# Strassen's seven products for eight in the second layer's first product, its split weights kept in HBM

## The chip, the cores and the metric

One core of a Trainium2 chip runs the whole program. The metric is device time in microseconds from one launch to its end: the median of three runs was 867.01 us, the lowest 866.56, the highest 867.7. Beside these there is one profiled execution, whose trace has a span of 865.0 us.

## The reference, cut to what matters

```python
scores = scale * np.matmul(q, k.transpose(0, 1, 3, 2))          # 4 batches, 8 heads, 576 tokens, 64 wide
ret = scores * Dmat[None, :, :, :]                              # decay gamma ** (i - j) below the diagonal
x = np.matmul(ret, v) -> 2304 tokens x 512
h = x @ w_in;   g = np.maximum(0.01 * h, h);            x = g @ w_out      # first layer, 512 -> 2048 -> 512
h = x @ w_in2;  g = h * (1.0 / (1.0 + np.exp(-h)));     out = g @ w_out2   # second layer, same sizes
```

All is float32 (the weights arrive as float64). Each layer is two products of 2304 x 512 x 2048.

## The kernel before

Three stages follow one another on TensorE: retention for the eight units of `UNITS` (its small matmuls are woven into the first layer), the first layer, the second layer. Every large product is done in three passes (`PASSES`): each float32 operand is split into a high part `hi`, a rounded float32r copy written by ScalarE (line 113), and a low part, source minus `hi`, written by VectorE (line 114). The passes hi*hi, hi*lo and lo*hi are added in PSUM.

A layer goes through blocks of tokens (`BLOCKS`), and in a block through the 16 tiles `f` of 128 hidden units; one (block, f) is a step. In a step `gemm1` makes `h` (128 hidden units x n tokens) from 4 chunks of 128 inputs in 3 passes: 12 matmuls with n columns each. `activate` applies the nonlinearity and splits the result into `g`. Two steps later (`LAG`) `gemm2` multiplies it with the second weight matrix into `acc`. In the first layer the output is transposed (hidden weights stationary, n columns); in the second layer `g` is stationary and each matmul has 512 columns of weights: 3 passes for each 128 tokens, 12 in a step of 512 tokens. The second layer's blocks are four of 512 tokens and one of 256.

The weights are split again for each block (`split_wi`, `split_wo`), from float32 copies `wraw` that stay in SBUF. These come from the float64 input by `load_w` (two DMAs of 512 KB for one f) and `decode` (ScalarE line 369, VectorE lines 374, 384 and 390). The second layer's weights are loaded and decoded during the last block of the first layer.

The order on every engine is written out by hand up to step 32 (`tc.manual_schedule()`); from there a list scheduler of the framework orders every engine's instructions. PSUM has eight banks: two for `ps` (the tiles `h`), four for `acc`, two for `att`. All DMAs are issued from SyncE's one queue, in order.

Of the kernel before, what the change touches and what calls it, by code (L numbers as in the profile page):

```python
# [21 lines left out]
W2 = 26  # L22
# [5 lines left out]
FIXED = 2 * NF  # L28
CA, CB = 256, S - 256
# [13 lines left out]
for _u in UNITS:  # L43
    POS[_u] = _p
    _p += CA if _u[0] == "A" else CB
BLOCKS = [[(0, 512), (512, 320), (832, 512), (1344, 512), (1856, 448)],
          [(0, 512), (512, 512), (1024, 512), (1536, 512), (2048, 256)]]
# [15 lines left out]
def retention_mlp_kernel(ctx: ExitStack, tc: tile.TileContext, qkva, qkvb, w1, w2, consts, out):  # L63
    nc = tc.nc

    def pool(name, bufs, space=None):
        kw = {"space": space} if space is not None else {}
        return ctx.enter_context(tc.tile_pool(name=name, bufs=bufs, **kw))

    const = pool("const", 1)  # L70
    wraw_p = pool("wraw", 16)
    wi_p = pool("wi", 2)
    wo_p = pool("wo", 2)
    x_p = pool("x", 1)
    xs_p = pool("xs", 6)
    hs_p = pool("hs", 2)
    g_p = pool("g", 3)
    ld_p = pool("ld", 3)
    dec_p = pool("dec", 3)
    pt_p = pool("pt", 4)  # L80
    y_p = pool("y", 2)
    st_p = pool("st", 4)
    acc_p = pool("acc", 1, PSUM)
    att_p = pool("att", 1, PSUM)
    ps_p = pool("ps", 2, PSUM)

# [13 lines left out]
    mask2 = wraw_p.tile([128, H, 128], F32, tag="wraw", name="mask2")  # L100
# [33 lines left out]
    def mm(out, lhsT, rhs, start, stop):  # L134
        return nc.tensor.matmul(out, lhsT, rhs, start=start, stop=stop)  # L135
# [13 lines left out]
    def load(u, p):  # L149
# [6 lines left out]
        if u in UNITS[:2]:  # L156

            t = wraw_p.tile([128, m], F32, tag="wraw", name="qkvk")
# [185 lines left out]
    def load_w(layer, f, parts=(0, 1)):  # L344

        if (layer, f) not in w64:
            p, tag = (ld_p, "ld") if layer == 1 and f < 2 else (wraw_p, "wraw")
            wraw[layer, f] = p.tile([128, 1024], F32, tag=tag, name="wraw")
            w64[layer, f] = dec_p.tile([128, 1024, 2], I32, tag="w64", name="w64")
# [77 lines left out]
    def activate(layer, i, f):  # L427
# [6 lines left out]
        if layer == 0:  # L434
            yield nc.scalar.activation(out=hs[:, :n], in_=h[:, :n], func=AF.Prelu, alpha=0.01)  # L435
        else:
            yield nc.scalar.activation(out=hs[:, :n], in_=h[:, :n], func=AF.Sigmoid)  # L437
            yield nc.vector.tensor_tensor(out=hs[:, :n], in0=h[:, :n], in1=hs[:, :n], op=ALU.mult)  # L438
        yield from split(g[:, 0, :n], g[:, 1, :n], hs[:, :n], nc.vector)

    def gemm2(layer, i, f):
        p0, n = BLOCKS[layer][i]
        nt = KC if layer == 0 else n // 128
        if f == 0:
            t = [acc_p.tile([128, 2, 512], F32, tag=f"acc{m}", name=f"acc{m}") for m in range(2)]

            acc[layer, i] = [t[m // 2][:, m % 2] if nt > 2 else t[m][:, 0] for m in range(nt)]
        g, w = gs[layer, i, f], wsp[layer, i, f, 1]
        for m in range(nt):
            a = acc[layer, i][m]  # L450
            ms = slice(m * 128, (m + 1) * 128)
            for wa, ga in PASSES:
                st = f == 0 and (wa, ga) == (0, 0)
                sp = f == NF - 1 and (wa, ga) == PASSES[-1]
                if layer == 0:
# [134 lines left out]
    for t, (l, i, f) in enumerate(steps):  # L590
# [53 lines left out]
        else:  # L644
# [3 lines left out]
            if t + 2 < len(steps):  # L648
                run(split_wi(*steps[t + 2]))
# [77 lines left out]
```

## Time and profile before

| | |
|---|---|
| median of 3 runs | 867.01 us (866.56 to 867.7) |
| span of the profiled execution | 865.0 us |
| TensorE busy | 855.0 us, 5736 matmuls |
| VectorE busy | 538.0 us |
| ScalarE busy | 443.7 us |
| granted TensorE clock | 0.999 |
| read from HBM, written | 53.11 MB, 4.72 MB |

The chain of waits is the one to start with: it follows the end of the program back, and says which engine held it up. Then the groups of instructions by shape give the number of matmuls, and the timeline gives the distance between the starts of two runs of them, which is what one costs in a stream: the mean duration of a matmul overlaps with the next. The same holds for VectorE and ScalarE: an instruction of 0.69 us may be followed by the next one after 0.60 us.

### The profile page before, as it was taken

The numbers are of one execution on the slowest core, as the hardware profiler recorded it, in microseconds if no ns is written. First come the engines' busy times: TensorE is split into PE (matmuls) and PEld (weight loads), VectorE is DVE, ScalarE is ACT, GpSimd is POOL, SyncE is SP. The second block draws the span as 40 slices with busy tenths as digits, with TensorE's granted clock in tenths as the row PEclk, the third lists the DMA queues.
The fourth block names the chain that finished last, engine by engine and source line by source line (L and its number), as shares of the span: only waits on it lengthen the run. The fifth ranks groups of instructions, "written<-read, shape, count | busy, mean of one in ns | idle before, by whom it ended". The sixth has DMA issues, their size and how long they took to land.

```text
span 865.0 us, 14049 instructions
## 1 busy us (share of the span) xinstructions
PE 855.0 (99%) x5736; PEld 714.8 (83%) x5736; DVE 538.0 (62%) x909; ACT 443.7 (51%) x769; POOL 17.1 (2%) x34
## 2 busy tenths in 40 slices
PE   8999999999999999999999999999999999999998
PEld 5678889998877878889998888888888888888897
DVE  6898856675454564548998444654465446544575
ACT  3788744454343444456666444544454445444564
POOL 5100000000000000000000000000000000000000
PEclk9999999999999999999999999999999999999999
DMA  9767532111111020102660000000001000100000
GB/s 342 275 217 258 168 109 90 58 66 58 50 57 66 1 82 1 49 1 97 231 207 1 2 0 1 25 25 0 1 21 29 1 0 12 38 1 0 25 26 25
DMA packets 17824, 58.73 MB, mean 68 GB/s; under 512 B 2016, under 2 KB 2144, under 8 KB 17760
## 3 DMA queue, kind: packets, MB, share of 16 engines
q1 hardware_dynamic: 17760, 57.83, 19.0%
q8 instruction: 45, 0.74, 0.3%
q14 instruction: 19, 0.16, 0.1%
HBM read 53.11 MB, written 4.72 MB: 67 GB/s over the span
## 4 chain that ended last, share of the span: by engine, by line
PE 93%; DVE 1%; ACT 0%; issue 0%
PE acc L135 45%; PE h L135 44%; PE o L135 2%; PE r L135 2%; DVE st L279 0%; DVE y L471 0%; DVE g L114 0%; ACT g L113 0%; DVE wi L114 0%; DVE wo L114 0%; ACT hs L435 0%; DVE xs L114 0%; DVE pt L204 0%; ACT xs L113 0%; DVE wraw L387 0%
## 5 line engine op out<-in xcount | busy, mean ns | idle before, releaser
L135 PE MATMUL h<-xs,wi 128*128 128x512 f32 (+3 forms) x1920 | 429.6, 370 | 1.8 <-ACT wi L113 1.1
L135 PEld LDWEIGHTS h<-xs,wi 128*128 128x128 f32 x1920 | 340.5, 188 | 62.1 <-ACT wi L113 2.1
L135 PE MATMUL acc<-g,wo 128*128 128x512 f32 (+2 forms) x960 | 216.1, 371 | 0.2 <-DVE wo L114 0.2
L135 PE MATMUL acc<-wo,g 128*128 128x512 f32 x864 | 209.9, 389 | 0.0
L135 PEld LDWEIGHTS acc<-g,wo 128*128 128x128 f32 x960 | 171.8, 188 | 27.0 <-DVE wo L114 0.6
L135 PEld LDWEIGHTS acc<-wo,g 128*128 128x128 f32 x864 | 161.0, 188 | 32.6
L113 ACT CAST wo<-wraw 128x512 fp32r<-128x512 f32 x160 | 99.5, 622 | 116.9 <-PE acc L135 115.8
L114 DVE TENSOR_TENSOR wo<-wraw,wo 128x512 fp32r<-128x512 f32 x160 | 110.4, 690 | 78.5 <-ACT wo L113 77.9
L114 DVE TENSOR_TENSOR wi<-wraw,wi 128x512 fp32r<-128x512 f32 x158 | 108.5, 686 | 56.4 <-ACT wi L113 54.3
L438 DVE TENSOR_TENSOR hs<-h,hs 128x512 f32<-128x512 f32 (+1 forms) x80 | 51.1, 639 | 119.0 <-ACT hs L437 118.9
L114 DVE TENSOR_TENSOR g<-hs,g 128x512 fp32r<-128x512 f32 (+3 forms) x160 | 101.6, 635 | 15.3 <-ACT g L113 10.6
L437 ACT ACTIVATE hs<-h 128x512 f32<-128x512 f32 (+1 forms) x80 | 44.5, 556 | 129.7 <-PE h L135 129.4
L113 ACT CAST wi<-wraw 128x512 fp32r<-128x512 f32 x160 | 98.2, 614 | 13.4 <-DVE wraw L390 13.4
L113 ACT CAST g<-hs 128x512 fp32r<-128x512 f32 (+3 forms) x160 | 93.6, 585 | 15.3 <-DVE hs L438 14.7
L435 ACT ACTIVATE hs<-h 128x512 f32<-128x512 f32 (+2 forms) x80 | 44.3, 553 | 101.0 <-PE h L135 100.1
L369 ACT ACTIVATE wraw<-w 128x1024 f32<-128x1024 f32 (+1 forms) x35 | 36.9, 1059 | 19.4 <-DVE wo L114 12.0
L374 DVE TENSOR_SCALAR w<-w 128x512 uint16<-128x512 uint32 (+1 forms) x34 | 35.7, 1051 | 9.0 <-ACT wraw L369 8.2
L390 DVE SCALAR_TENSOR_TENSOR wraw<-w,wraw 128x1024 int32<-128x1024 int32 (+1 forms) x35 | 39.6, 1131 | 1.3 <-ACT w L380 0.7
L113 ACT CAST xs<-X 128x512 fp32r<-128x512 f32 (+3 forms) x42 | 22.9, 561 | 3.4 <-DVE X L322 2.3
L114 DVE TENSOR_TENSOR xs<-X,xs 128x512 fp32r<-128x512 f32 (+3 forms) x38 | 22.9, 618 | 2.4 <-ACT xs L113 2.2
L380 ACT ACTIVATE w<-w,seven 128x512 uint16<-128x512 uint32 x14 | 20.5, 1463 | 0.0
L384 DVE TENSOR_SCALAR wraw<-wraw 128x512 int32<-128x512 int32 (+1 forms) x34 | 20.1, 590 | 0.0
(57 smaller groups left out, 233.5 us busy)
## 6 DMA issues: line engine op xcount, KB each, us to landing
w<-in_w SPq DMA_DIRECT2D x64, 512.0 KB, 4.7
qkv<-in_qkvb SPq DMA_DIRECT2D x16, 672.0 KB, 6.3
qkvk<-in_qkva SPq DMA_DIRECT2D x16, 256.0 KB, 5.4
qkv<-in_qkva SPq DMA_DIRECT2D x8, 512.0 KB, 4.2
out<-y SPq DMA_DIRECT2D x15, 256.0 KB, 2.0
out<-y SPq DMA_DIRECT2D x6, 128.0 KB, 2.3
cst<-in_consts SPq DMA_DIRECT2D x1, 150.0 KB, 2.3
```

The costliest lines, as they stand in the source:

```text
L113: yield nc.scalar.copy(out=hi, in_=src)
L114: yield engine.tensor_tensor(out=lo, in0=src, in1=hi.bitcast(F32), op=ALU.subtract)
L135: return nc.tensor.matmul(out, lhsT, rhs, start=start, stop=stop)
L369: yield nc.scalar.mul(out=w, in_=hi.bitcast(F32), mul=2.0 ** -112)
L374: yield nc.vector.tensor_scalar(out=end[:, c], in0=lo[:, c].bitcast(U32), scalar1=2.0 ** -29, scalar2=7.0, op0=ALU.mult, op1=ALU.min)
L380: yield nc.scalar.activation(out=end[:, c], in_=lo[:, c].bitcast(U32), func=AF.Relu, scale=-2.0 ** -29, bias=seven)
L384: nc.vector.tensor_scalar(out=wi[:, c], in0=wi[:, c], scalar1=3, scalar2=None, op0=ALU.logical_shift_left)
L390: yield nc.vector.scalar_tensor_tensor(out=wi, in0=hi, scalar=-0x7FFFFFF9, in1=wi, op0=ALU.bitwise_and, op1=ALU.bitwise_xor)
L435: yield nc.scalar.activation(out=hs[:, :n], in_=h[:, :n], func=AF.Prelu, alpha=0.01)
L437: yield nc.scalar.activation(out=hs[:, :n], in_=h[:, :n], func=AF.Sigmoid)
L438: yield nc.vector.tensor_tensor(out=hs[:, :n], in0=h[:, :n], in1=hs[:, :n], op=ALU.mult)
```

## The change

The second layer's first product is done on pairs of 384 tokens (three pairs, `PAIRS`) and pairs of hidden tiles (k = 0 to 7, each two tiles f). The 512 inputs are two halves. That is a product of 2x2 blocks by 2x2 blocks, which needs eight block products in the plain way; the change does it in seven, by the Winograd form of Strassen's scheme. A block product is 2 chunks x 3 passes = 6 matmuls of 384 columns (`product`), so a pair k takes 42 of them (`quad`) where the plain way would take 48.

Four sums of token blocks (`sums_x`, for each pair of token blocks) and four sums of weight blocks (`sums_w`, once for each k) are new, and seven split token operands and seven split weight operands. The split weights of all k, and the split second weights, are written to a scratch tensor in HBM (`kept`, 2.88 MB for each k) while the first pair of token blocks is worked on, and read back for the other two pairs (`fetch`, `weights_out`).

The four results are made in two PSUM tiles, `a` and `b`: after the first, second and third product of the chain in `a`, ScalarE copies it out (`snapshot`) and VectorE adds `b` to the copy (`add`); `finish` applies Silu in place of Sigmoid and a product, and splits. Between the block products the matmuls of the second product of the pair before are placed (`left`, one group of three matmuls for each 128 tokens; `yield 3` means three such groups). In the first quad there are none.

The outputs of a pair (6 tiles of 128 tokens) are gathered in six banks. PE's and SP's order is written out by hand in the second layer, the others' is the scheduler's. The second layer's weights come later: seven f during the last seven steps of the first layer, the other nine during the first pair. Pools are opened and closed so that the new tiles take the place of old ones.

```diff
+TILE = 384
+PAIRS = B * S // (2 * TILE)
-          [(0, 512), (512, 512), (1024, 512), (1536, 512), (2048, 256)]]
...
+    def sums_x(p):
+        t1, t2, t4 = (xt_p.tile([128, 2, TILE], F32, tag="xt", name="xt") for _ in range(3))
+        yield nc.vector.tensor_tensor(out=t1, in0=b12, in1=b11, op=ALU.subtract)
...
+        for name, x in (("b11", b11), ("b21", b21), ("t2", t2), ("t1", t1), ("t3", b12), ("t4", t4), ("b22", b22)):
+            yield nc.scalar.copy(out=hi, in_=x)
+            yield nc.vector.tensor_tensor(out=lo, in0=x, in1=hi.bitcast(F32), op=ALU.subtract)
...
+    dram = pool("scratch", 1, bass.MemoryType.DRAM)
+    kept = {k: dram.tile([128, 22, 256], F32, tag=f"kept{k}", name="kept") for k in range(NF // 2)}
+    PARTS = (("ha", 0, 3), ("la", 3, 3), ("hs", 6, 4), ("ls", 10, 4))
...
+    def weights_out(p, k):
+            if p:
+                nc.sync.dma_start(out=here, in_=there)
+            else:
+                yield from split(wo[i][:, 0], wo[i][:, 1], wraw[1, 2 * k + i][:, 512:], nc.vector)
+                nc.sync.dma_start(out=there, in_=here)
+
+    def fetch(p, k):
+        for n, o, m in PARTS:
+            nc.sync.dma_start(out=t[n].bitcast(F32), in_=kept[k][:, o:o + m])
...
+    def sums_w(p, k):
+        yield nc.scalar.copy(out=ha[:, :2], in_=a)
+        yield nc.vector.tensor_tensor(out=la[:, :2], in0=a, in1=ha[:, :2].bitcast(F32), op=ALU.subtract)
+        yield nc.vector.tensor_tensor(out=s1, in0=z[:, :256], in1=z[:, 256:512], op=ALU.add)
+        yield nc.vector.tensor_tensor(out=s2, in0=s1, in1=w[:, :256], op=ALU.subtract)
+        yield nc.scalar.copy(out=hs[:, :2], in_=s[0])
+        yield nc.vector.tensor_tensor(out=ls[:, :2], in0=s[0], in1=hs[:, :2].bitcast(F32), op=ALU.subtract)
...
+        for n, o, m in PARTS:
+            nc.sync.dma_start(out=kept[k][:, o:o + m], in_=t[n].bitcast(F32))
+
+    def product(out, p, k, a, b, start, stop):
+        w, x = ww[p, k, a], xw[p, b]
+        for c in range(2):
+            for i, (e, f) in enumerate(PASSES):
+                mm(out, w[e][:, c * 128:(c + 1) * 128], x[f][:, c], start and c == 0 and i == 0,
+                   c == 1 and i == len(PASSES) - 1, skip_group_check=True)
+
+    def finish(p, k, f, t, h):
+        with tc.high_priority():
+            nc.scalar.activation(out=g, in_=h, func=AF.Silu)
+            nc.scalar.copy(out=hi, in_=g)
+            nc.vector.tensor_tensor(out=lo, in0=g, in1=hi.bitcast(F32), op=ALU.subtract)
...
+    def quad(p, k):
+        product(a, p, k, "a11", "b11", True, False)
+        c11 = snapshot()
+        product(b, p, k, "a12", "b21", True, True)
+        add(c11)
+        finish(p, k, 0, 0, c11)
+        yield 3
+        product(a, p, k, "s2", "t2", False, False)
+        c12 = snapshot()
+        yield 2
+        product(b, p, k, "s1", "t1", True, False)
+        product(a, p, k, "s3", "t3", False, False)
+        c22 = snapshot()
+        add(c22)
+        finish(p, k, 1, 1, c22)
+        yield 3
+        product(a, p, k, "a22", "t4", False, True)
+        finish(p, k, 1, 0, a)
+        product(b, p, k, "s4", "b22", False, True)
+        add(c12)
+        finish(p, k, 0, 1, c12)
+        yield 4
...
+    later.enter_context(tc.manual_schedule(engines={mybir.EngineType.PE, mybir.EngineType.SP}))
+    for p in range(PAIRS):
+        for k in range(NF // 2):
+            if after[0] == 0:
+                more = sums_w(*after)
+            elif after[0] < PAIRS:
+                fetch(*after)
...
+            if p == 0:
+                more_weights(nw + (2 if k < 4 else 1))
+            left = outputs(p, k)
```

ScalarE at the turn from the first layer to the second. Before, the table of Sigmoid is loaded and the step goes on as the steps before it (`hs<-h` is the nonlinearity, `wi`, `wo` and `g` are the hi copies of splits, `X<-acc` an eviction of the first layer):

```order
L113 CAST wo<-wraw 128x512
L437 ACT_TABLE_LOAD
L437 ACTIVATE hs<-h 128x512
L113 CAST wi<-wraw 128x512
L113 CAST wo<-wraw 128x512
L113 CAST g<-hs 128x512
L437 ACTIVATE hs<-h 128x512
```

Now (`X<-a` is a snapshot, or where it is ACTIVATE a Silu that reads PSUM; `X<-X` is Silu on a copy; `gh` is the hi part of the result):

```order
L581 COPY X<-a 128x384
L566 ACT_TABLE_LOAD
L566 ACTIVATE X<-X 128x384
L467 COPY X<-acc_4178 128x448
L567 CAST gh<-X 128x384
L467 COPY X<-acc_4179 128x448
L121 CAST wo<-wraw 128x512 x4
L581 COPY X<-a 128x384 x2
L566 ACTIVATE X<-X 128x384
L567 CAST gh<-X 128x384
L566 ACTIVATE X<-a 128x384
L567 CAST gh<-X 128x384
```

The second and third snapshot of the first quad stand behind the table load, two evictions of the first layer and four copies of second weights.

TensorE at the same place. Before, runs of 12 matmuls of either product alternate in the second layer:

```order
L135 MATMUL h<-xs,wi 128x512 x12
L135 MATMUL acc_5505<-wo,g 128x512 x6
L135 MATMUL acc_5506<-wo,g 128x512 x6
L135 MATMUL h<-xs,wi 128x512 x12
L135 MATMUL acc_5505<-wo,g 128x512 x6
```

Now, in the first quad (`a`, `b`: block products; `xh`, `xl` and `ha`, `la`, `hs`, `ls`: hi and lo of token and weight operands; `acc<-g,wo`: the last of the first layer):

```order
L143 MATMUL b<-xl,ha 128x384
L143 MATMUL acc_4178<-g,wo 128x448 x2
L143 MATMUL acc_4179<-g,wo 128x448 x2
L143 MATMUL b<-xh,la 128x384
L143 MATMUL acc_4178<-g,wo 128x448 x4
L143 MATMUL acc_4179<-g,wo 128x448 x4
L143 MATMUL a<-xh,hs 128x384
L143 MATMUL a<-xl,hs 128x384
L143 MATMUL a<-xh,ls 128x384
```

From the product on `a` that begins there, 30 matmuls of block products follow with no others between them, then the second quad's first 12.

VectorE in the loaded part. Before, in the last block of the first layer, a decode (lines 374, 384, 390) stands between the lo parts of the splits:

```order
L114 TENSOR_TENSOR g<-hs,g 128x448
L374 TENSOR_SCALAR w_4907<-w_4907 128x1024
L384 TENSOR_SCALAR wraw<-wraw 128x1024
L114 TENSOR_TENSOR wo<-wraw,wo 128x512
L390 SCALAR_TENSOR_TENSOR wraw<-w_4907,wraw 128x1024
L374 TENSOR_SCALAR w_4989<-w_4989 128x1024
L384 TENSOR_SCALAR wraw<-wraw 128x1024
L114 TENSOR_TENSOR wi<-wraw,wi 128x512
```

Now, in the fourth quad of the first pair, from one `add` (line 586) to the next (`ws` are sums of weights, `la` lo parts of weights, `gl` lo parts of results; lines 381, 391 and 397 a decode):

```order
L586 TENSOR_TENSOR X<-b,X 128x384
L538 TENSOR_TENSOR ws<-wraw 128x256
L542 TENSOR_TENSOR ws<-wraw 128x256
L381 TENSOR_SCALAR w_5077<-w_5077 128x1024
L391 TENSOR_SCALAR wraw<-wraw 128x1024
L568 TENSOR_TENSOR gl<-X,gh 128x384
L547 TENSOR_TENSOR la<-wraw,ha 128x256
L539 TENSOR_TENSOR ws<-ws,wraw 128x256
L122 TENSOR_TENSOR wo<-wraw,wo 128x512
L568 TENSOR_TENSOR gl<-X,gh 128x384
L397 SCALAR_TENSOR_TENSOR wraw<-w_5077,wraw 128x1024
L586 TENSOR_TENSOR X<-b,X 128x384
```

Ten instructions of other work stand between two adds for which TensorE waits.

## Rows read from the trace of the kernel before

**Rows 1.** Page: busy time by engine; clock and bandwidth in 40 slices

```profile
PE 855.0 (99%) x5736; PEld 714.8 (83%) x5736; DVE 538.0 (62%) x909; ACT 443.7 (51%) x769; POOL 17.1 (2%) x34
...
PEclk9999999999999999999999999999999999999999
...
GB/s 342 275 217 258 168 109 90 58 66 58 50 57 66 1 82 1 49 1 97 231 207 1 2 0 1 25 25 0 1 21 29 1 0 12 38 1 0 25 26 25
```

**Rows 2.** Page: the chain that ended last, share of the span by engine

```profile
PE 93%; DVE 1%; ACT 0%; issue 0%
```

**Rows 3.** Groups by shape, TensorE: busy us, mean ns; idle before

```profile
L135 PE MATMUL h<-xs,wi 128*128 128x512 f32 x1344 | 329.4, 392 | 1.6 <-ACT wi L113 1.1 <-DVE xs L114 0.5
L135 PE MATMUL acc<-wo,g 128*128 128x512 f32 x864 | 209.9, 389 | 0.0
L135 PE MATMUL h<-xs,wi 128*128 128x256 f32 x192 | 25.8, 282 | 0.0
```

**Rows 4.** Timeline, TensorE, second layer: start us, us, engine, line, shapes, count

```profile
484.02 2.88 PE L135 MATMUL h<-xs,wi 128*128 128x512 f32 x12
486.74 2.88 PE L135 MATMUL acc<-wo,g 128*128 128x512 f32 x12
489.46 2.88 PE L135 MATMUL h<-xs,wi 128*128 128x512 f32 x12
```

**Rows 5.** Timeline, TensorE, blocks of 448 and of 256 tokens

```profile
394.66 5.03 PE L135 MATMUL h<-xs,wi 128*128 128x448 f32 x24
399.52 0.77 PE L135 MATMUL acc<-g,wo 128*128 128x448 f32 x3
...
838.48 1.59 PE L135 MATMUL h<-xs,wi 128*128 128x256 f32 x12
839.91 1.55 PE L135 MATMUL acc<-wo,g 128*128 128x512 f32 x6
841.30 1.59 PE L135 MATMUL h<-xs,wi 128*128 128x256 f32 x12
```

**Rows 6.** Timeline, VectorE, last block of the first layer

```profile
434.75 1.34 DVE L374 TENSOR_SCALAR w<-w 128x1024 uint16<-128x1024 uint32 x1
435.88 0.73 DVE L384 TENSOR_SCALAR wraw<-wraw 128x1024 int32<-128x1024 int32 x1
436.53 0.67 DVE L114 TENSOR_TENSOR wo<-wraw,wo 128x512 fp32r<-128x512 f32 x1
437.12 1.21 DVE L390 SCALAR_TENSOR_TENSOR wraw<-w,wraw 128x1024 int32<-128x1024 int32 x1
```

**Rows 7.** Groups by shape, VectorE and ScalarE

```profile
L114 DVE TENSOR_TENSOR wi<-wraw,wi 128x512 fp32r<-128x512 f32 x158 | 108.5, 686 | 56.4 <-ACT wi L113 54.3
L204 DVE TENSOR_TENSOR pt<-r,mask 128x384 f32<-128x384 f32 x16 | 8.8, 553 | 0.7 <-PE r L135 0.7
L438 DVE TENSOR_TENSOR hs<-h,hs 128x256 f32<-128x256 f32 x16 | 6.8, 424 | 6.9 <-ACT hs L437 6.8
...
L437 ACT ACTIVATE hs<-h 128x256 f32<-128x256 f32 x16 | 6.2, 385 | 10.5 <-PE h L135 10.5
```

**Rows 8.** Busy time by engine in stretches of 10 us; clock, DMA share, GB/s

```profile
413.00:423.00 10.00, 10.00 (x51) 9.28 (x50) 9.47 (x13) 6.55 (x11) 0.00 (x0) 1.00 0.80 283
433.00:443.00 10.00, 10.00 (x51) 9.27 (x50) 9.82 (x13) 6.30 (x10) 0.00 (x0) 1.00 0.64 218
```

**Rows 9.** Timeline, ScalarE, at the turn between the layers

```profile
463.69 1.28 ACT L437 ACT_TABLE_LOAD   x1
467.34 0.60 ACT L437 ACTIVATE hs<-h 128x512 f32<-128x512 f32 x1 [2.36 <-PE h L135]
467.83 0.61 ACT L113 CAST wi<-wraw 128x512 fp32r<-128x512 f32 x1
468.34 0.62 ACT L113 CAST wo<-wraw 128x512 fp32r<-128x512 f32 x1
```

**Rows 10.** Page: DMA issues, KB each, median us from issue to landing

```profile
w<-in_w SPq DMA_DIRECT2D x64, 512.0 KB, 4.7
...
out<-y SPq DMA_DIRECT2D x15, 256.0 KB, 2.0
```

More of the change, by code (lines that the diff above doesn't have):

```diff
@@ L85, in retention_mlp_kernel, with slot @@
     ps_p = pool("ps", 2, PSUM)
+    def slot(shape, dt, name, kind="wraw"):
+        return wraw_p.tile(shape, dt, tag=kind, name=name, bufs={"wraw": NF - 7, "first": 7}[kind])
     cst = const.tile([128, NC + NP * CH], F32, name="cst")
@@ L433, in activate @@
         gs[layer, i, f] = g
[L434 to L438, printed above, removed]
+        yield nc.scalar.activation(out=hs[:, :n], in_=h[:, :n], func=AF.Prelu, alpha=0.01)
         yield from split(g[:, 0, :n], g[:, 1, :n], hs[:, :n], nc.vector)
@@ new lines, in retention_mlp_kernel, with temp, snapshot, add @@
+    temps = itertools.cycle([X[:, c, i * TILE:(i + 1) * TILE] for c in range(2) for i in range(2)])
+    def temp():
+        return next(temps)
+    def quad(p, k):
+        def snapshot():
+            s = temp()
+            with tc.high_priority():
+                nc.scalar.copy(out=s, in_=a)
+            return s
+        def add(s):
+            with tc.high_priority():
+                nc.vector.tensor_tensor(out=s, in0=b, in1=s, op=ALU.add)
+        a = ps_p.tile([128, 512], F32, tag="ps", name="a")[:, :TILE]
+        b = ps_p.tile([128, 512], F32, tag="ps", name="b")[:, :TILE]
+        product(a, p, k, "a11", "b11", True, False)
[19 more added lines that the diff above has]
+        yield 4
@@ L644, in retention_mlp_kernel @@
         else:
-            if t >= t0 - 2:
-                more_weights(NF + 1 + (t - t0 + 2) * 15 // W2)
+            if t >= t0:
+                more_weights(NF + max(0, min(t - t0 - 6, NF - 9)))
                 decodes()
+            if t == t0:
+                heads.close()
+                xh_p = pool("xh", 7, side=right, stack=second)
+                xt_p = pool("xt", 3, side=right, stack=second)
+                x0 = sums_x(0)
+            if t >= t0 + 6:
+                for _ in range(3):
+                    next(x0, None)
+            if t == t0 + NF - 4:
+                run(x0)
+                w0 = sums_w(0, 0)
+            if t >= t0 + NF - 4:
+                for _ in range(4):
+                    next(w0, None)
             if t + 2 < len(steps):
```

177 lines of the change are left out of this document (135 added, 42 removed).

## The prediction

> **What bounds the kernel now.** I read the page's busy times first, then the chain of waits, then the groups by shape, and last the timelines of the stretches that give a price. TensorE is busy for 855.0 of 865.0 us, at the full granted clock in every slice [rows 1], and the chain that ended last lies on TensorE for 93% [rows 2]. A busy TensorE proves little by itself, since its matmuls overlap; the proof is in the groups and the timeline. The second layer's matmuls show next to no idle time before them: 0.0 us before the 864 of the second product, 1.6 us before all 1344 of the 512-column form of the first [rows 3]. And the starts stand at equal distances: runs of 12 begin at 484.02, 486.74 and 489.46, so a matmul of 512 columns costs 2.72 / 12 = 226.7 ns in the stream, whichever product it is of [rows 4]. So what is taken away from TensorE comes off the end, as long as nobody makes it wait.
>
> **What the change removes from TensorE.** Before, the first product of the second layer is 4 x 192 matmuls of 512 columns and 192 of 256. The latter cost (839.91 - 838.48) / 12 = 119.2 ns [rows 5]. 768 x 0.2267 + 192 x 0.1192 = 174.1 + 22.9 = 197.0 us. Now there are 3 pairs x 8 k x 42 = 1008 matmuls of 384 columns, a form that the trace doesn't show. It shows 448 columns at (399.52 - 394.66) / 24 = 202.5 ns and 256 at 119.2 [rows 5]; on the line between these two 384 is 174.7 ns, on the line between 256 and 512 it is 172.9. I take 174: 175.4 us, between 174.3 and 176.1. The gain is 21.6 us, give or take 1. The second product keeps its 864 matmuls of 512 columns. A quad (one pair, one k) is then 42 x 0.174 + 36 x 0.2267 = 7.31 + 8.16 = 15.47 us of TensorE, and the layer is 24 of them.
>
> [...]
>
> **What it adds, and what covers it.**
>
> *The start of the layer.* In the first quad there are no matmuls of a second product to lie between the block products, so each hand-over is open. I count from the end of the first block product (0). The second one ends at 1.85 us (6 x 0.174 and 4 of 448 columns between), 8 more of 448 follow to 3.5, then s2t2 to 4.5 and s1t1 to 5.55. The next, s3t3, writes on `a` and needs the second snapshot. On ScalarE this stands behind the first snapshot, the table load (1.28 us [rows 9]), Silu, which waits for the first add (2.5), two evictions, one gh and four copies of 512. A copy of 512 follows the next after 0.51 us [rows 9]; ACTIVATE on 384 is about 0.49, the middle of 0.385 for 256 and 0.60 for 512 [rows 7, 9], and 0.1 less when the next follows at once; Silu isn't in the trace and is taken as Sigmoid, which these rows are of. That gives Silu to 3.0, evictions and gh to 4.3, four copies to 6.4, the snapshot to 6.9: TensorE waits 1.35 us. After s3t3 (7.95) the third snapshot is open too: 0.55 us. a22t4 and s4b22 then run to 10.6. The second quad's weights `ha` stand on ScalarE behind two Silus and two gh, which puts them at 11.5 (0.9 us of waiting), and their lo part `la` on VectorE behind an add and a gl, at 12.45 (another 0.6). Together 3.4 us. Bounds: 1.5, if the scheduler's order leaves ScalarE ahead of where I put it, and 8, if each of the ten hand-overs costs 0.4 us more.
>
> *The last block of the first layer.* Seven decodes, the split of the first sums of tokens and the first two sums of weights now stand there. In its last eight steps (8 x 24 x 0.2025 = 38.9 us of TensorE) VectorE has seven decodes of 1.13 + 0.65 + 1.21 = 3.0 us [rows 6], 8 x (0.59 + 0.59 + 0.53) us of splits and some 5 us of sums: 39.7 us. So it is full. The block before the change was full as well, 9.82 of 10 us, with TensorE at 10.00 of 10 [rows 8]. I take 0.5 us, from 0 to 3.
>
> *The first pair, quads 2 to 8.* VectorE has for each quad four sums and one lo part of 256, three lo parts of 512, two of second weights, two decodes (in four of the quads), four gl and three adds of 384. By the distances between starts (0.59 for 512 [rows 6], and 0.1 under the mean durations 0.553 for 384 and 0.424 for 256 [rows 7]) that is 1.6 + 1.8 + 1.2 + 6.0 + 3.15 = 13.7 us; by the mean durations (0.686 for 512 [rows 7], 3.28 for a decode) it is 16.0. TensorE's quad is 15.47. So VectorE is 89% full if its work comes in a stream, and the bound if every instruction waits for the one before. TensorE asks for two adds in good time only: from the third block product to s1t1, and from the third snapshot to s4b22, there are some 3 us each. I take 1 us in all, from 0 to 12: the stretch of rows 8 is the nearest row, with TensorE unhurt beside a VectorE at 9.8 of 10. In pairs 2 and 3 the sums of weights and the decodes are gone and VectorE is at 7 us or less; the sums of the next pair's tokens (11 instructions of 768, about 0.87 us each by the same slope) come in one quad each, 3.15 + 9.6 us, and fit.
>
> *DMA.* The first pair writes 2.88 MB for each quad, and in four quads reads 2.10 MB of float64 weights beside it: 4.98 MB in 15.47 us, 322 GB/s. The next pairs read 2.88 MB, 186 GB/s. The trace shows 342 GB/s in the first slice [rows 1] and 283 GB/s at a share of 0.80 [rows 8], so some 350 at full load, all of it reading; writing shows only in pieces of 256 KB that land after 2.0 us [rows 10]. SP issues in order, and each quad's weight loads stand behind the stores of the sums. In quad 2 the first decode on ScalarE comes about when its load lands, with 1.83 MB of stores ahead of it, and a Silu for which TensorE waits stands behind it: 0.5 us, from 0 to 3. Later loads have some 9 us to spare: they are issued 8 us into a quad, and their decode stands 8 us into the next one.
>
> The Trainium skill's page "SBUF — State Buffer", section "The DMA setup-cost knee", speaks against stores of 0.39 and 0.52 MB: about 2 us go to each transfer besides its bytes. One after the other, six stores and four loads would take some 31 us by its figures, twice a quad, and the kernel would come to about 920 us. The trace does not agree that they queue so: 512 KB loads land after 4.7 us [rows 10], which in turn would be 112 GB/s, while 283 were moved [rows 8].
>
> *The end.* The last quad's second product has 36 matmuls with nothing between them, and the same two evictions and stores end the program. I count no change.
>
> **The sum.** 865.0 - 21.6 + 3.4 + 0.5 + 1.0 + 0.5 = 848.8 us of span. The median of the runs, 867.01, is 2.0 above the span of the profiled execution, so the forecast is 850.8, rounded to 851.0 us.
>
> **Rivals.**
> - *Nothing waits.* All stops but a fraction are hidden by the scheduler's order: 867.0 - 21.6 = 845.4 us. For it: the full VectorE of rows 8 cost nothing. Against it: the second snapshot stands behind work that I could name.
> - *VectorE becomes the bound of the first pair.* The adds stand in a strict order among the sums, and each of them waits for TensorE or for a ScalarE copy. With mean durations (16.0) and four waits of 0.5 us a quad takes 18 us, 2.5 more than TensorE; over five quads 12.5 us: 863 us. For it: ten instructions stand between two adds. Against it: rows 6 and 8.
> - *Slower: stores to HBM.* If writing goes at half the rate of reading (177 GB/s for 354), a quad of the first pair needs 2.88 / 0.177 + 2.10 / 0.354 = 22.2 us in four quads, 6.7 too many, and 16.3 in three: 29 us, less 9 to spare, 20: 871 us. ScalarE then waits at its decode for the load, and Silu and the snapshots behind it. It decides from a first pair 16 us longer than I say. For it: no row shows writing in bulk. Against it: the 2.0 us of the small stores.
>
> **How the numbers follow.** The forecast (847 to 856) has 0.54, no waiting 0.20, VectorE 0.16, the stores 0.10. What a measurement of this kernel can tell from no change is 0.2%, 1.7 us: faster is under 865.3, slower over 868.7. Faster: 0.54 + 0.20 + 0.12 of VectorE's 0.16 = 0.86. Slower: 0.08 of the stores' and 0.01 of VectorE's = 0.09. The rest, 0.05, is within. The range goes from 845.0, just under the case without waits, to 864.0, which holds most of VectorE's.
>
> **What would show it.** The block products' starts: 6 x 0.174 = 1.04 us from one run to the next, where nothing waits. TensorE's gaps: after s1t1 and s3t3 of the first quad and at the start of the second, 3.4 us together, the first two ended by ScalarE. Quads 3 to 8 at 15.5 us and those of pairs 2 and 3 at 15.5 without gaps. A first pair with quads of 17 us or more whose gaps are ended by VectorE would speak for that rival; ScalarE waiting at its decode for a load, or a median time to landing of the stores above 8 us, for the slower one. The granted clock should stay at 1.00: if it doesn't in the first quads, the stops were longer than worked out. It would be wrong from the ground up if a 384-column matmul cost 195 ns or more: then the gain is nothing.

## The result

The changed kernel takes 856.45 us (median of 4 runs, 855.64 to 858.67) against 866.96 us for the kernel before. The ratio is 0.988, with a 95% interval of 0.9866 to 0.9894. The forecast was 851.0 us, so the sign was right, the time lies in the range of 845.0 to 864.0, and the gain is 10.5 us where 16.0 were forecast. By the profiled executions it is 854.4 us of span where the sum said 848.8: 5.6 us too few. Most of this document is on where these 5.6 us are.

### The profile page after: what moved, and what is told of

It reads as the page before. It is cut to its first block, busy times and chain, and to the rows that moved or that the text cites. A ratio compares the mean times of both kernels' runs of the same rounds, so it can differ in the third digit from the quotient of the medians.

```text
span 854.4 us, 14185 instructions
## 1 busy us (share of the span) xinstructions
PE 837.3 (98%) x5784; PEld 724.2 (85%) x5784; DVE 479.2 (56%) x850; ACT 423.1 (50%) x762; POOL 16.8 (2%) x34
## 4 chain that ended last, share of the span: by engine, by line
PE 87%; DVE 3%; DMA 2%; ACT 1%; SPq 0%; issue 0%; DVEq 0%; ACTq 0%
PE acc L143 36%; PE h L143 21%; PE a L143 11%; PE b L143 8%; PE att L143 7%; PE o L143 2%; PE r L143 2%; DMA qkv<-in_qkvb 1%; DMA w<-in_w 1%; SPq L359 0%; DVE wraw L397 0%; DVE w L381 0%; DVE gl L568 0%; ACT wo L121 0%; DVE wo L122 0%
## 5 line engine op out<-in xcount | busy, mean ns | idle before, releaser
L143 PE MATMUL h<-xs,wi 128*128 128x512 f32 (+2 forms) x960 | 218.6, 373 | 2.5 <-ACT wi L121 1.7
L143 PEld LDWEIGHTS h<-xs,wi 128*128 128x128 f32 x960 | 171.0, 188 | 31.6 <-ACT wi L121 2.7
L143 PE MATMUL acc<-wo,gh 128*128 128x512 f32 x384 | 134.0, 390 | 0.0
L122 DVE TENSOR_TENSOR wi<-wraw,wi 128x512 fp32r<-128x512 f32 x78 | 53.7, 689 | 63.1 <-ACT wi L121 61.9
L143 PEld LDWEIGHTS acc<-wo,gh 128*128 128x128 f32 x384 | 72.1, 188 | 12.9
L568 DVE TENSOR_TENSOR gl<-X,gh 128x384 fp32r<-128x384 f32 x96 | 53.4, 556 | 45.4 <-ACT gh L567 45.4
L143 PE MATMUL acc<-wo,gl 128*128 128x512 f32 x192 | 75.3, 392 | 0.8 <-DVE gl L568 0.8
L143 PE MATMUL att<-wo,gh 128*128 128x512 f32 x192 | 70.8, 390 | 0.0
L122 DVE TENSOR_TENSOR g<-hs,g 128x512 fp32r<-128x512 f32 (+2 forms) x80 | 50.5, 631 | 9.2 <-ACT g L121 9.2
L567 ACT CAST gh<-X 128x384 fp32r<-128x384 f32 x96 | 49.1, 513 | 2.5
L376 ACT ACTIVATE wraw<-w 128x1024 f32<-128x1024 f32 (+1 forms) x35 | 36.8, 1055 | 10.5 <-DMA w<-in_w 6.3
```

The costliest lines, as they stand in the source:

```text
L122: yield engine.tensor_tensor(out=lo, in0=src, in1=hi.bitcast(F32), op=ALU.subtract)
L376: yield nc.scalar.mul(out=w, in_=hi.bitcast(F32), mul=2.0 ** -112)
L567: nc.scalar.copy(out=hi, in_=g)
L568: nc.vector.tensor_tensor(out=lo, in0=g, in1=hi.bitcast(F32), op=ALU.subtract)
```

## The profile after

The page of the changed kernel: busy time, clock and bandwidth in 40 slices, and the chain that ended last.

```profile
PE 837.3 (98%) x5784; PEld 724.2 (85%) x5784; DVE 479.2 (56%) x850; ACT 423.1 (50%) x762; POOL 16.8 (2%) x34
...
PEclk9999999999999999999999999999999999999999
...
GB/s 338 277 223 242 175 114 107 59 66 58 50 58 66 2 33 2 1 0 1 1 185 99 209 398 363 285 195 212 213 234 169 170 234 140 272 207 138 227 92 74
...
PE 87%; DVE 3%; DMA 2%; ACT 1%; SPq 0%; issue 0%; DVEq 0%; ACTq 0%
```

TensorE lost 17.7 us of busy time against [rows 1] and is the bound still, at the same clock. The chain lies on it for 87% where it was 93% [rows 2]. VectorE, the DMA and ScalarE have taken a few per cent of the chain. The layer's slices (the last 18) now move 138 to 398 GB/s, and 92 and 74 at the end, where all of them moved under 40.

The chain of waits of the changed kernel in one quad (start us, us, what):

```profile
521.99 1.36 PE acc L143 x6
523.35 1.05 PE a L143 x6
524.40 1.05 PE b L143 x6
525.46 1.38 PE acc L143 x6
526.83 1.36 PE att L143 x6
...
537.58 0.45 PE acc L143 x2
```

A block product of six 384-column matmuls costs 1.05 us. The mean distance from one start to the next, stops left out, is 175.4 ns over the whole layer; the line between [rows 5] had said 174. A quad is 537.58 - 521.99 = 15.59 us, where 15.47 was worked out. The products make up 42 x 0.1754 = 7.37 of it, and 8.22 us are left for 36 matmuls of 512 columns: 228.3 ns each, not the 226.7 of [rows 4]. Both are about 1% above the price taken. The lines show where the second comes from: six matmuls of 512 columns right behind a block product take 1.38 us, and the six behind those 1.36, which is the 226.7 ns of [rows 4].

Busy time of the changed kernel by engine in three quads of the first pair (PE, PEld, DVE, ACT, POOL; then clock, DMA share, GB/s), the answer to [rows 8]:

```profile
490.50:506.00 15.50, 14.71 (x74) 13.02 (x73) 13.55 (x22) 9.25 (x18) 0.00 (x0) 1.00 1.03 390
506.00:522.00 16.00, 16.00 (x81) 14.48 (x80) 14.81 (x24) 11.30 (x21) 0.00 (x0) 1.00 1.03 413
522.00:537.60 15.60, 15.60 (x79) 14.14 (x79) 14.44 (x25) 10.27 (x19) 0.00 (x0) 1.00 0.94 343
```

VectorE is up to 93% full and the DMA is at its limit, and yet TensorE has no gap in the second and third of these rows. Where it does stop in the whole layer is a short list. The changed kernel's timeline of TensorE, with the idle time before an instruction and its releaser in brackets, the neighbours of the first stop, and the last matmul of all:

```profile
472.57 0.34 PE L143 MATMUL b<-xh,ls 128*128 128x384 f32 x1
474.18 0.45 PE L143 MATMUL a<-xh,hs 128*128 128x384 f32 x1 [1.27 <-ACT X L581]
474.46 0.34 PE L143 MATMUL a<-xl,hs 128*128 128x384 f32 x1
...
476.07 0.45 PE L143 MATMUL a<-xh,ha 128*128 128x384 f32 x1 [0.57 <-ACT X L581]
479.22 0.44 PE L143 MATMUL a<-xh,ha 128*128 128x384 f32 x1 [0.78 <-ACT ha L534]
480.19 0.44 PE L143 MATMUL a<-xh,la 128*128 128x384 f32 x1 [0.36 <-DVE la L535]
502.18 0.50 PE L143 MATMUL acc<-wo,gl 128*128 128x512 f32 x1 [0.79 <-DVE gl L568]
...
847.70 0.39 PE L143 MATMUL att<-wo,gh 128*128 128x512 f32 x1
```

The first four stops are the hand-overs that the prediction named, in its order and with its releasers: second snapshot, third snapshot, `ha`, `la`. A stop costs more than its idle time. From 472.57 to 474.46 are 1.89 us, where two matmuls in the stream take 0.35: 1.54 us lost for 1.27 us of idle time. Idle time is counted from the end of the matmul before, 0.34 us after its start, while in the stream the next one starts after 0.175; and behind the stop the next start comes 0.28 us later. That is some 0.27 us for each stop, and the four stops cost 4.1 us for 2.98 us of idle time. The fifth stop is in the second quad. The changed kernel's chain of waits there begins at a weight slice that lands late:

```profile
484.32 6.57 DMA w<-in_w
...
490.98 1.14 ACT wraw L376
...
501.66 0.48 DVE gl L568
```

The slice was issued at 483.09 behind stores of the split sums, and its decode set VectorE's order back until `gl` came late. Transfers take longer than before; of the changed kernel's DMA issues (KB each, us to landing):

```profile
w<-in_w SPq DMA_DIRECT2D x64, 512.0 KB, 5.6
```

where the weight slices took 4.7 [rows 10]. At the end, the changed kernel's sync queue issues eight stores:

```profile
846.02 0.34 SPq L636 DMA_DIRECT2D out<-y  x1
846.74 1.11 SPq L636 DMA_DIRECT2D out<-X  x2
847.95 1.73 SPq L636 DMA_DIRECT2D out<-y  x3
849.77 0.54 SPq L636 DMA_DIRECT2D out<-X  x1
850.40 0.40 SPq L636 DMA_DIRECT2D out<-y  x1
```

and the kernel before issued two there:

```profile
861.31 0.89 SPq L476 DMA_DIRECT2D out<-y  x2
```

Before, the span ended 3.9 us after the last matmul (861.13 to 865.0); now it ends 6.3 us after it (848.1 to 854.4). VectorE's last eviction, in the changed kernel and in the kernel before:

```profile
848.74 0.69 DVE L465 COPY y<-att 128x512 f32<-128x512 f32 x1 [0.66 <-ACT X L467]
861.15 0.69 DVE L471 COPY y<-acc 128x512 f32<-128x512 f32 x1 [1.33 <-PE acc L135]
```

Now it waits for ScalarE's eviction of the other block in its PSUM tile and starts 0.6 us after the last matmul; before, it started right at the last matmul's end.

## The experiments

Theory: TensorE sets the pace of the layer, and the 5.6 us are in the price of a matmul, in stops at named places and in the end. Rivals: VectorE or ScalarE set the pace of the first pair; or the traffic to HBM costs time all along.

The first product of the layer starts between 462.9 and 464.7 us in the changed kernel and its variants (e3_vector left out, whose additions begin earlier), and its place is at 462.75 in the kernel before. So up to 2 us of a single profile are the run's own. For small effects I therefore also give the time from that start to the end of the span, which is 390.7 us for the changed kernel; it is called "the layer" below. The sets of runs were taken at different times, and the kernel before took 866.96 to 868.82 us beside them; so differences of 1 to 2 us between the medians of two sets rest on the traces, not on the times alone.

### e1_eighth: an eighth product

```diff
+        product(b, p, k, "s4", "b22", False, False)
         product(b, p, k, "s4", "b22", False, True)
```

> In each of the 24 quads the seventh product (s4 by b22) is done twice, so a quad has eight block products again; left as they are: the quad's sums, evictions and outputs (the output block it feeds holds that product twice). Theory (TensorE alone sets the quad's pitch, other engines follow): 24 quads x 6 matmuls x 0.175 us = 25.2 us more, about 881.6 us, quad pitch 15.59 + 1.05 = 16.64 us, and the stops at the start of the layer unchanged. Rival (VectorE, ScalarE or the DMA set the pace of quads 2 to 8, and TensorE had slack there that the profile does not show as idle time): the first 8 quads take little of it, 17 us or less in all, about 873 us.

879.77 us, 23.3 more than the changed kernel, and 1.4% above the kernel before (1.0124 to 1.0155). The quad's pitch, from one quad's start to the next, is 16.64 us (609.29 to 625.93 in its chain), as expected to the hundredth. The stop in the second quad is gone, presumably since the other engines now have 1 us more for each quad; at the start of that quad there is one stop of 0.89 us of idle time instead of two with 1.14 together; and the span ends 5.9 us after the last matmul instead of 6.3. With the stops at their full cost that is 25.2 - 1.1 - 0.4 = 23.7, and the layer grew by 23.8. The theory held: a block product more costs its full 1.05 us.

### e2_no_kept: no stores and reloads

```diff
-        for n, o, m in PARTS:
-            nc.sync.dma_start(out=kept[k][:, o:o + m], in_=t[n].bitcast(F32))
```

(the store of the output weights and all reloads go likewise)

> The split weights are neither stored in HBM nor reloaded; pairs 2 and 3 multiply with the split weights of the first pair's last two quads, so their part of the result uses other weights; every matmul, sum and eviction stays. Theory (the traffic is hidden except for the one stop of 0.79 us in the second quad, where a weight slice lands late): 0.5 to 1.2 us less, about 855.5 us; the stops at the start of the layer and the pitch of 15.59 us stay. Rival (stores and reloads take time from the matmuls all along, or hold back the end): 5 us or more less, 851 us or below.

867.93 us: 11.5 slower, which neither theory had. ScalarE's timeline of this kernel at the start of the layer:

```profile
467.70 1.13 ACT L376 ACTIVATE wraw<-w 128x1024 f32<-128x1024 f32 x1 [2.95 <-DMA w<-in_w]
...
472.92 1.13 ACT L376 ACTIVATE wraw<-w 128x1024 f32<-128x1024 f32 x1 [3.72 <-DMA w<-in_w]
...
479.12 0.47 ACT L575 COPY X<-a 128x384 f32<-128x384 f32 x1
```

With the sync queue empty, weight loads were issued at 462.13, 466.81 and 472.04 us, where the changed kernel issues the next one at 483.09, and the scheduler put their decodes into the first quad, ahead of the snapshots. ScalarE works in order, so the second snapshot (479.12, where it was 473.65) stood behind a decode that waited for its transfer, and TensorE stopped for 5.8 us; the clock fell behind the stop, which the last section shows. The run says nothing on the traffic: the edit changed the order on an engine that it didn't touch. It does show what the slower rival of the prediction described, ScalarE waiting at a decode with snapshots behind it.

### e3_vector: five more additions a quad

```diff
+            for _ in range(5):
+                yield nc.vector.tensor_tensor(
+                    out=spare, in0=wraw[1, 2 * k][:, :512], in1=wraw[1, 2 * k][:, 512:], op=ALU.add)
```

> Five more VectorE additions of 128 x 512 (about 0.6 us each, 3.0 us a quad, never read) in each of the first pair's eight quads. Theory (VectorE was busy 13.9 to 14.7 of 15.6 us in quads 2 to 5 and less later, with queues between it and TensorE): each of the full quads goes over by about 1.3 to 2.1 us, the later ones have room, and part is caught up: 3 to 10 us more, about 862 us, stops of TensorE on VectorE in quads 3 to 6. Rival 1 (an in-order VectorE already binds; all extra work is felt): 24 us more, about 880 us. Rival 2 (it has slack that the busy time hides, since the end of one instruction overlaps the start of the next): no change, 856.5 us.

869.02 us, 12.6 more: half of the 24 us of work came out at the end, above the theory's 3 to 10. TensorE stopped for 7.6 us in all on the sums, the longest time here:

```profile
533.80 0.56 PE L143 MATMUL b<-xh,hs 128*128 128x384 f32 x1 [2.90 <-DVE X L586]
```

and it ran at a lower clock after two of the stops (0.78 of full in 475.0 to 490.5, 0.89 in 522.0 to 537.6). So VectorE isn't the bound, but it has little to spare in the full quads. The scheduler again chose where the additions stand (four of them between the first quad's first sum and its second), so the 12.6 is not a pure price of VectorE's time.

### e4_twice: each store made twice

```diff
             nc.sync.dma_start(out=kept[k][:, o:o + m], in_=t[n].bitcast(F32))
+            nc.sync.dma_start(out=again[k][:, o:o + m], in_=t[n].bitcast(F32))
```

(and likewise for the output weights)

> Every store of split weights to HBM is made twice, the second time into another tensor that is never read: 2.1 to 2.9 MB more in each quad of the first pair. Theory (the DMA was at its limit in quads 2 and 3, 390 to 413 GB/s with a busy share of 1.02 and 1.03, and new weight slices queue behind the stores): slices land late, ScalarE is held by the decode, TensorE stops: 8 to 25 us more, 865 to 881 us. Rival (the share counts waiting, the rate has room; what costs is the latency of one landing): less than 2 us more.

878.77 us, 22.3 more, in the theory's range. From 490 to 584 us the DMA moves 366 to 417 GB/s at a share of 1.01 to 1.03, as the changed kernel's does in two quads; so that is about the ceiling of this mixed traffic, and the changed kernel reaches it in two of these six quads. But the place was not the one expected. From 490 to 538 us TensorE shows no stop at all, and it stops later, 15.4 us at six places between 549 and 600 us:

```profile
549.80 0.69 PE L143 MATMUL a<-xh,hs 128*128 128x384 f32 x1 [3.24 <-ACT hs L542]
```

The releasers are VectorE's and ScalarE's sums of weights, not a decode that waits for its slice. Behind these stops the clock fell too (0.77 of full from 569 to 584 us), which is part of the 22.3. The sync queue issues one quad's weight loads from 524.72 and the next quad's from 544.63, 19.9 us apart where TensorE needs 15.6 for a quad, so the queue falls behind. What holds each single sum I can't read from the trace: the chain goes back from VectorE over landings of the copies (11.1 and 8.8 us from issue), and that stays open. What the run shows is that this traffic has no room to double.

### e5_start: the copies of the output weights behind the snapshots

```diff
-                yield from split(wo[i][:, 0], wo[i][:, 1], wraw[1, 2 * k + i][:, 512:], nc.vector)
+                for j, y in enumerate(split(wo[i][:, 0], wo[i][:, 1], wraw[1, 2 * k + i][:, 512:], nc.vector)):
+                    if j == 0 and k < 2:
+                        behind(y, marks[2 if k == 0 else 5])
+                    yield y
```

(`marks` holds the snapshots and the gh copies in order: 2 is the second snapshot, 5 the third gh; in the first quad this work is also handed to the scheduler four steps later)

> The changed kernel, with the ScalarE copies of the first two quads' output weights (four of them, 2.19 us, which stood ahead of the second snapshot) put behind the second snapshot and behind the first quad's third g; nothing else is done or left out. Theory (the stop of 1.27 us at the second snapshot is four copies that stand ahead of it in an in-order queue; the three smaller stops of 0.57, 0.78 and 0.36 us come from other work): the 1.27 us go, with the 0.1 us that TensorE's queue takes to refill, the three others stay: 1.0 to 1.6 us less, about 855.1 us. Rival (ScalarE has too much to do here altogether, and the copies only move the stop to a later one): less than 0.4 us less, the stop on the a11 weights of the second quad grows by what the first loses.

856.59 us: no change. The stop of 1.27 us is gone, so its cause was as stated; that a queue refills behind a stop, as the expectation has it, no run shows. But the time came back in the second quad, where TensorE now waited 1.13, 0.34 and 0.66 us. VectorE's timeline there:

```profile
481.69 1.28 DVE L122 TENSOR_TENSOR wo<-wraw,wo 128x512 fp32r<-128x512 f32 x2
482.89 0.55 DVE L590 TENSOR_TENSOR X<-b,X 128x384 f32<-128x384 f32 x1
```

The second quad's output weights, now copied later, stand ahead of the first quad's last sum, and g and gl follow that sum. The rival was right in effect, though not on `ha`, whose stop stayed at 0.78.

### e6_end and e7_both: the end in another order

```diff
-                    if k == NF // 2 - 1 and f == 1 and n % 2:
-                        for e in (n - 1, n):
+                    if final and f == 1 and (n % 2 or p == PAIRS - 1):
+                        for e in (n,) if p == PAIRS - 1 else (n - 1, n):
```

(with the loop order t, f in the last quad; e7_both joins this to the edit of e5_start)

> The changed kernel, with the last quad's outputs in another order: both weight blocks of the first 384 tokens, then of the second, and each 128-token block evicted and stored when it is done, so that three blocks of six are stored before the last 4 us and one is left at the end; same matmuls, same stores. Theory (the span ends 6.3 us after the last matmul instead of 3.9 us as before the change, since eight stores of 0.33 to 0.59 us each stand in the sync queue at the end): 1.5 to 2.4 us less, about 854.5 us, and the span ends about 4 us after the last matmul. Rival (the last stores are slow because HBM or the queue is, and the one that ends last takes as long): 0.5 us or less.

> Both edits, of the start and of the end. Theory: the two gains add up, 2.5 to 4 us less than the changed kernel, about 853.2 us. Rival (either one shifts the other's order): the better of the two alone.

857.44 and 858.37 us: no gain, the layer 1.1 and 2.0 us longer. The waits of TensorE in e6_end have two new rows (us in total, times, longest):

```profile
PE acc L143 <- ACT y L467: 1.4, 2, 0.7
...
PE att L143 <- ACT X L467: 0.7, 1, 0.7
```

Two blocks share one PSUM tile; evicting the first as soon as it is done makes the matmuls of the second wait for the eviction. In e6_end the span did end 4.3 us after the last matmul instead of 6.3, as the theory said, but the last matmul came later.

### e8_no_traffic: no traffic, with the order held

```diff
-        yield nc.scalar.mul(out=w, in_=hi.bitcast(F32), mul=2.0 ** -112)
+        y = nc.scalar.mul(out=w, in_=hi.bitcast(F32), mul=2.0 ** -112)
+        if snaps:
+            behind(y, snaps[-1])
+        yield y
```

(beside the edit of e2_no_kept; in the first pair the decodes are also handed to the scheduler three steps later)

> Again without the stores to HBM and the reloads (pairs 2 and 3 multiply with the weights of the first pair's last two quads), and this time each weight slice's decode on ScalarE is held behind the third snapshot of its quad, so that no snapshot stands behind a decode that waits for its transfer, as it did for 5.8 us in the run without stores. Theory (the HBM traffic costs the stop of 0.79 us in the second quad and no more): 0.3 to 1.2 us less than the changed kernel, about 855.6 us, no stop over 1.5 us. Rival 1 (the traffic slows TensorE all along): 5 us or more less. Rival 2 (the first run without stores was slower for a reason other than the order on ScalarE): 865 us or more.

857.0 us, no change (the layer 0.4 longer). ScalarE's order at the start is that of the changed kernel, the four stops there are as before, and the time of e2_no_kept is gone with its stop: the second rival falls. With 133 GB/s in place of 390 to 413, a block product still costs 1.05 us and six of 512 columns 1.36: the first rival falls too. The stop in the second quad is gone, and the theory's 0.3 to 1.2 us were given back by a new order on VectorE. Four quads, from 489.48 to 553.13 us, now take 15.91 us each instead of 15.59, since in each of them TensorE waits for a gl that comes late (532.75 to 532.99 and 548.63 to 548.90 in the chain). So the traffic costs 1.1 us or less, the full cost of that stop.

### e9_end: the end mended

```diff
-                                nc.sync.dma_start(out=out[r:r + ln], in_=y[a:a + ln])
+                                (nc.sync if p < PAIRS - 1 or e % 2 else nc.scalar).dma_start(
+                                    out=out[r:r + ln], in_=y[a:a + ln])
```

(with the loop order of e6_end, evictions in pairs as in the changed kernel)

> The changed kernel with another end, mended after the first try: the last quad's outputs run both weight blocks of the first 384 tokens first and then those of the second, evictions stay in pairs (two blocks of one PSUM tile, so that no matmul waits for an eviction of its own tile), and the stores of the three blocks that ScalarE evicts are issued from ScalarE's queue instead of the sync queue. Theory (the end is 2.4 us longer than before the change because eight stores stand in one queue): 1 to 2 us less than the changed kernel, about 855.0 us, last matmul to end about 4.5 us instead of 6.3. Rival (the last landing takes its time whatever stands ahead of it): less than 0.4 us less.

855.31 us, 1.1 less than the changed kernel, in the theory's range; the runs of the two overlap, but the layer is 1.1 shorter too, and the end is 5.3 us after the last matmul instead of 6.3. The edit changes the loop order and the queue together; by the trace it is the queue, since the last store is issued 0.4 us after the last eviction (848.84 to 849.25) where it was 1.4 (849.43 to 850.80). The other 1.4 us to the kernel before are not a matter of one queue. 0.6 of them are VectorE's last eviction, which still waits for ScalarE's and starts at 848.15, 0.65 us after the last matmul; 0.8 are the landing of the last store, 3.0 us after its issue where it was 2.1 before. Why it lands later is open.

### e10_early and e11_all: the loads a quad earlier

```diff
                 coming = itertools.chain(*(decode(*x) for x in now))
+                more_weights(nw + (2 if k < 4 else 1))
...
-            if p == 0:
-                more_weights(nw + (2 if k < 4 else 1))
```

(with the decodes held as in e8_no_traffic; e11_all joins this to the edits of e5_start and e9_end)

> The changed kernel with the weight loads of each of the first pair's quads issued ahead of that quad's stores in the sync queue, one quad earlier than now, and each decode held on ScalarE behind the snapshot issued last before it. Theory (the stop of 0.79 us in the second quad is a slice that lands late since its load stood behind stores; an earlier load takes it away): 0.5 to 1 us less, about 855.7 us, no stop in quads 2 to 8. Rival (the order on VectorE decides, and holding the decodes only makes other small stops, as the 0.33 us per quad in the second run without traffic): no change within 0.5 us, stops of 0.2 to 0.5 us on the gl or the sums in quads 2 to 6.

> The three edits together: the output weights' copies behind the snapshots, the loads a quad earlier, the mended end. Theory (with the slices there in time, the 1.5 us won at the start are no longer given back in the second quad): 3 to 4 us less than the changed kernel, about 853 us. Rival (ScalarE's and VectorE's work of the first two quads binds, and the stop moves again): the gain of the end alone, about 855 us.

e10_early: 856.96 us, no change. The late slice and its stop are gone, and four waits of 0.24 to 0.3 us on VectorE's sums have come, 1.2 us in all, as its rival said. e11_all: 853.95 us, 2.5 less than the changed kernel, where the theory said 3 to 4. The stop of 1.13 us on gl, the one that e5_start had made, is still there; so earlier loads don't cure it.

### e12_later: one dependency moved

```diff
-                        behind(y, marks[2 if k == 0 else 5])
+                        behind(y, marks[2 if k == 0 else 8])
```

(8 is the second quad's first gh)

> The three edits again, with one dependency moved: the copies of the second quad's output weights, which stood on ScalarE and VectorE ahead of the last sum of the first quad (1.28 us of VectorE), now come behind the second quad's first g. Theory (the stop of 1.13 us in the second quad is VectorE's two subtractions of these weights, ahead of the sum and the gl that TensorE waits for): that stop falls to 0.2 us or less and nothing else moves, 0.8 to 1.3 us less than with the three edits, about 852.9 us. Rival (ScalarE and VectorE have too much to do in the first two quads, whatever the order): a stop of about the same size comes elsewhere in quads 2 or 3, no change.

852.77 us (5 runs, 852.1 to 852.8), 1.2 less than e11_all (the layer 387.2 us after 388.8) and 3.7 less than the changed kernel; 0.9827 of the kernel before (0.9813 to 0.984). All waits of TensorE in the second layer are now:

```profile
PE a L143 <- ACT ha L541: 0.8, 1, 0.8
PE a L143 <- ACT X L588: 0.6, 1, 0.6
PE a L143 <- DVE la L542: 0.4, 1, 0.4
```

The stop was VectorE's two subtractions, and no other came in its place: VectorE and ScalarE have room enough in the first two quads, and it was the order. This version beats both kernels.

## Why the prediction came out as it did

What bounds the kernel was right: e1_eighth shows that a block product more comes out at the end in full. The measured 856.45 us lie just above the 847 to 856 of the forecast proper, in the part of the range that was kept for VectorE as the bound; but the traces show no such bound, only terms that were too small. The terms, one by one:

| term | forecast, us | measured, us | from |
|---|---|---|---|
| gain on TensorE | 21.6 | 19.2 | 24 quads at 15.59 are 374.2; the layer's matmuls before, 393.3 |
| start of the layer | 3.4 | 4.1 | four stops: idle 2.98, and 4 x 0.27 |
| last block of the first layer | 0.5 | 0 | TensorE 10.00 of 10 beside VectorE at 10.00 |
| VectorE, quads 2 to 8; decode in quad 2 | 1.5 | 1.3 | one stop, 0.79 + 0.28, and 0.2 in two late starts at 485 |
| end | 0 | 2.4 | 6.3 after the last matmul, 3.9 before |
| before the change acts | 0 | 0.9 | first product at 463.69, 462.75 before |

(393.3: from 462.75 to the last matmul's place in the stream, 860.94, less 24 matmuls of the first layer at 0.2025.) The differences are 2.4 + 0.7 - 0.5 - 0.2 + 2.4 + 0.9 = 5.7, and 5.6 are to be explained; the rest is rounding.

- *The gain on TensorE* was mis-sized. 174 ns for 384 columns is 175.4, 0.06 us in a quad. And the 226.7 ns for 512 columns, read from runs of twelve in a stream of 512-column matmuls, hold only there: worked out from the starts in the trace, the first three behind a block product take 231 to 232 ns, and all behind them 226.7. A quad has four such places, another 0.06 us. 1% on one quad is little; on 24 quads it is 2.9 us, of which 0.5 stood in the kernel before as well (the mean of all its 512-column matmuls in the layer is 227.0 ns).
- *The start* was right in places and releasers, and 0.7 us too small: 1.35, 0.55, 0.9 and 0.6 us were forecast, and at their full cost the four stops are 1.54, 0.85, 1.04 and 0.63. e5_start and e12_later show that the largest stop was the order of the copies, not work that had to be there.
- *VectorE* as the bound (rival 2) fell: 13.6 to 14.8 us of busy time in stretches of 15.5 to 16 cost no more than the one stop. It was close all the same, as e3_vector shows, and every new order of its queue (e5_start, e8_no_traffic, e10_early) made small stops of up to 1.1 us.
- *The stores* (rival 3) fell: the DMA moved 390 to 413 GB/s of writing and reading mixed, not a lower rate for writing. The prediction's 350 for full load was too low: the 342 it starts from is the mean of a whole slice. e4_twice shows what more of them would have cost.
- *The stop in the second quad* was forecast at 0.5 and cost 1.1, by the mechanism that the chain shows, a load behind stores, though it was a gl and not a Silu that came late. The order on VectorE has a part in it: in e4_twice, with twice the stores ahead of the load, there is no stop at this place.
- *The end* is the step that failed: "the same two evictions and stores end the program. I count no change." The changed order evicts six blocks in the last 4.1 us where the kernel before left two, and eight stores of 0.33 to 0.59 us each stand in one in-order queue. e9_end took 1.0 of the 2.4 us back by using a second queue. Of the other 1.4, 0.6 are the two last evictions standing one behind the other, and 0.8 a later landing of the last store, whose cause is open.
- *The 0.9 us before the layer* belong to no edit: the last block's first matmul, which stands ahead of the work that changed, already starts at 385.26 instead of 384.32, and among the variants the first product starts anywhere from 462.9 to 464.7.

## What to carry to other kernels

Removing work from the bounding engine pays in full, but price the removed and the remaining instructions in the mixture that they will run in: 1% on a stage repeated 24 times was two fifths of the error. Count a stop at more than its idle time. Read the last few microseconds of the new order as a stage of its own, down to the number of stores that stand in the last queue and the evictions that share a tile. Where a scheduler sets the order of in-order engines, an edit on one engine moves work on others: two subtractions ahead of a sum cost 1.1 us of idle time, a decode ahead of a snapshot 11.5 us in all, and added dependencies took each away.

## What the hardware showed that I had not expected

A stop of several microseconds can cost far more than its length. In e2_no_kept the granted clock stood at full speed, TensorE then did next to nothing for 5.83 us (to 479.64), and the clock was at half, the lower of its two levels (1.2 instead of 2.4 GHz), for the next 15 us. The busy time of that kernel in stretches (PE first, the clock after POOL):

```profile
468.00:473.00 5.00, 4.30 (x23) 3.80 (x22) 3.54 (x4) 1.28 (x3) 0.00 (x0) 1.00 0.57 203
473.00:479.00 6.00, 0.81 (x5) 0.49 (x3) 4.60 (x6) 5.97 (x10) 0.00 (x0) 0.86 0.54 175
479.00:484.00 5.00, 3.79 (x11) 3.29 (x12) 4.59 (x8) 2.14 (x4) 0.00 (x0) 0.50 0.62 210
484.00:489.00 5.00, 3.40 (x11) 2.70 (x9) 4.50 (x7) 4.14 (x8) 0.00 (x0) 0.50 0.60 182
489.00:494.00 5.00, 4.03 (x12) 3.70 (x12) 5.00 (x10) 4.90 (x10) 0.00 (x0) 0.50 0.90 305
494.00:499.00 5.00, 5.00 (x24) 4.12 (x23) 5.00 (x9) 2.31 (x5) 0.00 (x0) 0.96 0.37 146
```

TensorE had three more stops, of 0.57 to 1.60 us of idle time, while the clock was low. The stops of 0.36 to 1.27 us of the changed kernel left it at 1.00.

The first three 512-column matmuls behind a run of 384 columns take 4 to 6 ns more than the 226.7 of a stream of 512 columns. The kernel before has the same behind the 256-column runs of its last block (233 to 236 ns for the first two), and nothing of it between 553 and 811 us, where all columns are 512. The cause isn't shown.

Writing to HBM and reading from it at the same time went at up to 413 GB/s, with block products at the same 1.05 us. Reading alone reaches the same rate: 398 GB/s at a share of 1.04 from 5 to 25 us of the kernel before, when nothing is written. The 342 of [rows 1] is lower only because its slice begins with 5 us at 166 GB/s.
